# The third quarter of the output weights goes through row sums of 512 columns, and their spread follows behind it

## Chip, cores and metric

The kernel runs on one core of a Trainium2 chip. The metric is the device time of one execution in microseconds (us); less is better. Before the change the median of three runs is 381.85 us (381.62 to 381.86).

## The reference

One token `x` (1024 values) goes through two blocks, and a scalar gate mixes them:

```python
g = sigmoid((x * gate_w).sum(-1))
q = (x @ wq)                       # 32 heads of 128
scores = q @ k_cache^T * 128**-0.5 # 4 key heads, 65536 keys, 8 query heads to each
o = softmax(scores) @ v_cache      # 32 x 128 = 4096 values
a = o @ wo                         # wo: 4096 x 1024
z = gelu(x @ w_in)                 # 3584 values: z1, z2
b = (z1 * (w_sp * layernorm(z2) + b_sp)) @ w_out   # w_out: 1792 x 1024
out = g * a + (1 - g) * b          # 1024 values, bf16
```

Keys and values are 64 MB each, `wo` is 8 MB (4096 x 1024 in bf16), `wq` 8 MB, `w_in` 7 MB, `w_out` 3.5 MB. Every byte is read once.

## The kernel before

All large operands come through one ring of SBUF memory, filled by one queue of transfers that SyncE (SP) issues in the order of the list `stream`: `wq`, keys, `w_in`, keys, `w_out`, then values and keys in turn, the last values, and at the end the output weights. A load is issued as soon as the data that it overwrites has been used (`done` calls `issue`, L376 to L400). The output weights come in six loads: the first three quarters `("wo", 0..2, 0)` of 2 MB each, and the fourth quarter cut by `WO_CUT` (L357) into pieces of 5, 2 and 1 of its 8 rows per partition (1280, 512 and 256 KB).

Order on each engine is the order in which the program records its operations; a helper class counts semaphores and puts a wait ahead of an operation that needs another engine's or a transfer's result. Nothing reorders the work afterwards. What all TensorE (PE) matmuls have in common is the helper `mm` (L257): the first matmul on given weights has line L260 in the profile, and those that use the same weights again have L262.

Keys are transposed by VectorE (DVE, L502) and multiplied on PE; scores, exponentials (ScalarE, ACT) and products with values follow for pairs of pieces. Behind the last values only the tail is left (L760 to L776). It makes the product of the 4096 attention values with `wo`, on top of what the other block has left in the same sums. Four names matter in it:

- `wo_rows(i)` multiplies quarter `i` in the form of *row sums*: the attention values are the stationary operand, one column of 128 at a time, and 512 columns of `wo` move past. There are 8 columns of values in a quarter and two halves of 512, so 16 matmuls. Column group `j = c % 4` of the array writes PSUM row `32 * j`, so four matmuls on different groups can run side by side. The result is four partial rows of 1024 in the PSUM tile `scp` (first half, key `KSC(0)`); they are accumulated over the calls.
- `spread(scp, ...)` adds these four rows and lays the 1024 sums out as 8 rows of 128 in the PSUM tile `fb` (named `fbt` in the profile): one ACT copy from `scp` to SBUF (L656), and then 8 matmuls with a selecting operand in f32 (L660), each of which the profile shows as two.
- `wo_piece(i, c0, c1)` multiplies rows of quarter `i` directly into the layout of `fb`: for each of its columns of values 8 matmuls of 128 moving columns (L712), so 64 for a whole quarter.
- `spin(n)` is `n` matmuls of 128 x 512 whose result in the other half of `scp` nobody reads.

The tail in the order recorded on PE is: the last values (`pv_piece(15)`), the softmax sums `out_first(3)`, `wo_rows(0)`, the last head group's scaling `out_rest(3)`, `wo_rows(1)`, `spin(4)`, `spread`, `spin(3)`, `wo_piece(2)`, `spin(3)`, and the three pieces of `wo_piece(3)`. Then DVE casts `fb` to bf16 (L775), and SP stores 2 KB (L366).

Of the kernel before, what the change touches and what calls it, by code (L numbers as in the profile page):

```python
# [138 lines left out]
def bass_gated_mix__gqa_block_cached__mixer_gmlp__decode_kernel(  # L139
# [64 lines left out]
    def ab(name, n, o=0):  # L204
        return arena[:, OFF[name] + o:OFF[name] + o + n]
# [51 lines left out]
    def mm(e, loaded, *a, **kw):  # L257

        if not loaded:
            return e.matmul(*a, **kw)  # L260
        with nc.discard():
            one = e.matmul(*a, **kw).ins  # L262
        return e.add_instruction(dataclasses.replace(one, name=nc.get_next_instruction_name(), ldweights=False))
# [129 lines left out]
    def use(key):  # L393
        n, off, w = place[key]
        assert n < issued[0], key
        return arena[:, OFF["RING"] + off:OFF["RING"] + off + w], [("slot", x) for x in grains(off, w)]

    def done(key):
        used.add(key)
        issue()  # L400
# [253 lines left out]
    def spread(src, keys, first):  # L654
        part = ab("KT", 2048, 4096).bitcast(F32)
        P("ACT", lambda e: e.activation(part[0:97, :], src[0:97, 0:1024], ACTF.Copy), w=[("kt", 1)] + keys)  # L656

        def f(e):
            for s, b, j in SLOTS:
                ins = e.matmul(fb[32 * b:32 * (b + 1), 0:QW], e4z[0:97, 31 - j:63 - j], part[0:97, QW * s:QW * (s + 1)],  # L660
                               start=(first and s % (NW // 2) == 0), stop=False, tile_position=(0, 32 * b),
                               skip_group_check=True)
            return ins
        P("PE", f, r=["e4", ("kt", 1)], w=["fb"])
# [17 lines left out]
    def spin(n):  # L682
        def f(e):
            for k in range(n):
                ins = mm(e, k > 0, scp[:, 1024:1536], idb, ab("KT", 512), start=True, stop=True)
            return ins
        P("PE", f, r=["idb", ("kt", 0)], w=[KSC(1)])

    def wo_rows(i):
        sl, keys = use(("wo", i, 0))  # L690

        def f(e):
            for c in range(8):
                j = c % 4
                z = 31 + 32 * (8 * i + c)
                for s in range(2):
                    o = DO * c + 512 * s
                    ins = mm(e, s > 0, scp[32 * j:32 * j + 1, 512 * s:512 * (s + 1)], ovz[:, z:z + 1], sl[:, o:o + 512],
                             start=(i == 0 and c < 4), stop=(i == 1 and c >= 4), tile_position=(0, 32 * j),
                             skip_group_check=True)  # L700
            return ins
        P("PE", f, r=[("ovec", i)] + keys, w=[KSC(0)])
        done(("wo", i, 0))

    def wo_piece(i, c0=0, c1=8):
        sl, keys = use(("wo", i, c0))
        def f(e, i=i, sl=sl, c0=c0, c1=c1):
            for c in range(c0, c1):
                for s, b, j in SLOTS:
                    o = DO * (c - c0) + QW * s  # L710
                    z = 31 + 32 * (8 * i + c) - j
                    ins = e.matmul(fb[32 * b:32 * (b + 1), 0:QW], ovz[:, z:z + 32],  # L712
                                   sl[:, o:o + QW], start=False, stop=(i == 3 and c == 7),
                                   tile_position=(0, 32 * b), skip_group_check=True)
            return ins
        P("PE", f, r=[("ovec", i)] + keys, w=["fb"])
        done(("wo", i, c0))
# [48 lines left out]
    out_rest(3)  # L766
    wo_rows(1)
    spin(4)
    spread(scp, [KSC(0)], False)
    spin(3)  # L770
    wo_piece(2)
    spin(3)
    for c0, c1 in WO_CUT:
        wo_piece(3, c0, c1)
# [34 lines left out]
```

## Time and profile before

| What | Value |
|---|---|
| Runs | 381.62, 381.86, 381.85 us, median 381.85 |
| Span of the profiled execution | 380.3 us |
| Median of the runs less that span | 1.55 us |
| Busy share: PE, DVE, ACT | 62%, 54%, 6% |
| Transfer engines: mean rate, share of time with packets of the load queue | 426 GB/s, 98.9% |
| Start of the tail's cast L775 | 378.79 us |

The page does not give the whole time of the profiled execution, only its span from first to last instruction; the runs beside it lie 1.3 to 1.5 us above it. The chip's TensorE has a clock that a throttle grants, shown as a share of full speed: in this profile it is either 1.0 or 0.5, and the mean over the span is 0.838. Times below are us from the start of the span. A line of the windows view gives the stretch and its length, the busy us and instructions of each engine in it, and at the end the granted clock, the busy share of the transfer engines and their rate.

### The profile page before, as it was taken

How to read it: one execution, taken by the hardware profiler on the slowest of the kernel's cores; microseconds unless marked ns; L12 is line 12 of the kernel's file. 1: busy time of each engine (PE TensorE's matmuls, PEld its weight loads, DVE VectorE, ACT ScalarE, POOL GpSimd, SP SyncE). 2: the span in 40 equal slices, each digit the busy share in tenths (PEclk: the TensorE clock that was granted, in tenths of full speed). 3: DMA queues.
4: the chain of work that ended last, by engine and by line, in shares of the span. 5: the costliest groups of instructions: out<-in, count | busy, mean ns of one | idle time of the engine just before them, and what ended most of it. 6: DMA issues, size and time to landing. Idle time of an engine off the chain costs nothing.

```text
span 380.3 us, 2581 instructions
## 1 busy us (share of the span) xinstructions
PE 235.1 (62%) x1449; PEld 58.1 (15%) x836; DVE 204.6 (54%) x162; ACT 23.3 (6%) x24; POOL 8.4 (2%) x37
## 2 busy tenths in 40 slices
PE   0061388458558924895788138952895884739378
PEld 0010011011111200122112001220121110212015
DVE  4011496778389525965892249745774882312020
ACT  1000000010420000002200000022000000220000
POOL 5000000000000000000000000000000000000000
PEclk9998599696859985998699859995899697958689
DMA  9999999999999999999999999999999999999996
GB/s 435 427 420 400 469 388 438 441 469 431 401 414 441 441 443 427 434 410 424 477 441 434 434 434 414 415 441 441 434 407 433 445 441 441 436 403 424 419 426 262
DMA packets 4254, 162.17 MB, mean 426 GB/s; under 512 B 532, under 2 KB 532, under 8 KB 788
## 3 DMA queue, kind: packets, MB, share of 16 engines
q1 hardware_dynamic: 4208, 162.01, 98.9%
q8 instruction: 9, 0.15, 0.2%
q10 hardware_dynamic: 36, 0.00, 0.0%
q14 instruction: 1, 0.01, 0.0%
HBM read 162.01 MB, written 0.00 MB: 426 GB/s over the span
## 4 chain that ended last, share of the span: by engine, by line
DMA 56%; PE 23%; DVE 18%; ACT 1%; issue 1%; SPq 0%; ACTq 0%; DVEq 0%
DMA arena<-in_A_k_cache_dram 34%; DVE arena L502 15%; DMA arena<-in_A_wo_dram 10%; DMA arena<-in_A_v_cache_dram 8%; PE scp L260 7%; PE scp L262 6%; DMA arena<-in_B_b_sp_dram 5%; PE obt L260 4%; PE obt L262 4%; DVE arena L539 1%; PE fbt L712 1%; PE fbt L660 1%; ACT arena L534 1%; SPq L389 0%; ACTq L288 0%
## 5 line engine op out<-in xcount | busy, mean ns | idle before, releaser
L502 DVE STREAM_TRANSPOSE arena<-arena 128x2048 f32<-128x2048 f32 x64 | 143.0, 2284 | 48.2 <-DMA arena<-in_A_k_cache_dram 32.7
L260 PE MATMUL scp<-arena 128*128 128x512 bf16 (+1 forms) x275 | 112.8, 429 | 87.7 <-DVE arena L502 86.3
L262 PE MATMUL scp<-arena 128*128 128x512 bf16 (+1 forms) x279 | 113.1, 427 | 0.0
L260 PE MATMUL obt<-arena 128*64 128x512 bf16 (+2 forms) x334 | 62.9, 419 | 17.5 <-DMA arena<-in_A_v_cache_dram 17.5
L262 PE MATMUL obt<-arena 128*64 128x512 bf16 (+2 forms) x334 | 62.2, 414 | 0.0
L260 PEld LDWEIGHTS scp<-arena 128*128 128x128 bf16 (+1 forms) x275 | 27.7, 104 | 200.1 <-issue 101.3
L539 DVE STREAM_TRANSPOSE arena<-arena 128x2048 bf16<-128x2048 bf16 x7 | 16.2, 2311 | 28.5 <-PE obt L262 26.4
L534 ACT ACTIVATE arena<-arena 128x2048 bf16<-128x2048 f32 x8 | 16.0, 2002 | 218.6 <-DVE arena L531 195.6
L260 PEld LDWEIGHTS obt<-arena 128*64 128x64 bf16 (+1 forms) x334 | 18.3, 113 | 70.7 <-issue 56.1
L519 DVE TENSOR_SCALAR_CACHE_REDUCE arena<-scp 128x2048 f32<-128x2048 f32 x8 | 18.3, 2292 | 16.0 <-PE scp L262 16.0
L580 PE MATMUL mbt<-arena 128*128 128x128 bf16 x16 | 1.9, 258 | 12.6 <-DVE arena L575 12.6
L542 DVE STREAM_TRANSPOSE arena<-arena 128x1024 bf16<-128x1024 bf16 x2 | 2.5, 1246 | 12.7 <-PE obt L262 12.7
L490 POOL COPY arena<-arena 32x32 bf16<-32x32 bf16 x16 | 3.2, 203 | 234.5 <-PE scp L262 209.7
L568 DVE RECIPROCAL arena<-mbt 128x1 f32<-128x1 f32 x4 | 0.6, 139 | 14.1 <-PE mbt L563 14.1
L531 DVE TENSOR_REDUCE arena<-mbt 128x1 f32<-128x32 f32 x4 | 0.8, 192 | 13.5 <-PE mbt L528 13.5
L437 PE MATMUL mbt<-arena 1*128 1x2 bf16 x1 | 0.2, 158 | 12.3 <-DMA arena<-in_B_b_sp_dram 12.3
L439 DVE COPY arena<-mbt 128x2 f32<-128x2 f32 x1 | 0.2, 160 | 12.3 <-PE mbt L437 12.3
L775 DVE CAST arena<-fbt 36x128 bf16<-36x128 f32 x1 | 0.3, 283 | 11.0 <-PE fbt L712 11.0
L432 PE MATMUL scp<-arena 8*128 8x1 bf16 x8 | 0.7, 199 | 8.7 <-DVE arena L427 8.7
L712 PE MATMUL fbt<-arena 128*32 128x128 bf16 x128 | 4.1, 220 | 0.1
L712 PEld LDWEIGHTS fbt<-arena 128*32 128x32 bf16 x128 | 3.6, 97 | 1.6 <-DMA arena<-in_A_wo_dram 0.8
L467 DVE CAST arena<-obt 97x1024 bf16<-97x1024 f32 x1 | 1.2, 1225 | 4.9 <-PE obt L262 4.9
(91 smaller groups left out, 54.2 us busy)
## 6 DMA issues: line engine op xcount, KB each, us to landing
arena<-in_A_k_cache_dram SPq DMA_DIRECT2D x6, 4096.0 KB, 33.1
arena<-in_A_v_cache_dram SPq DMA_DIRECT2D x2, 4096.0 KB, 26.0
arena<-in_B_w_in_dram SPq DMA_DIRECT2D x1, 7168.0 KB, 30.4
arena<-in_A_wo_dram SPq DMA_DIRECT2D x3, 2048.0 KB, 33.4
arena<-in_B_w_out_dram SPq DMA_DIRECT2D x1, 3584.0 KB, 21.5
arena<-in_A_wo_dram SPq DMA_DIRECT2D x1, 1280.0 KB, 30.3
arena<-in_A_wo_dram SPq DMA_DIRECT2D x1, 512.0 KB, 31.0
arena<-in_A_wo_dram SPq DMA_DIRECT2D x1, 256.0 KB, 30.8
```

What stands on the lines that cost most here:

```text
L260: return e.matmul(*a, **kw)
L262: one = e.matmul(*a, **kw).ins
L467: P("DVE", lambda e: e.tensor_copy(psb[0:97, :], ob[0:97, :]), w=["psb", "ob"])
L490: P("POOL", lambda e, pb=pb: e.tensor_copy(vw(qpad, 24 + 32 * pb, [[QP, 4], [1, 8]], 32 * pb, 32), vw(qall, 8 * g, [[32, 4], [1, 8]], 32 * ...
L502: P("DVE", lambda e: e.transpose(ktb(i).bitcast(F32), sl[:, 4096 * p:4096 * (p + 1)].bitcast(F32)), r=keys[4 * p:4 * p + 4], w=[("kt", i % ...
L519: P("DVE", lambda e: e.tensor_scalar(scs(j), scp[:, :], 0.0, None, op0=ALU.add, op1=ALU.max, accum_out=maxc[:, j:j + 1]), w=[("sc", j % 2) ...
L534: P("ACT", lambda e: e.activation(psb2, scs(j), ACTF.Exp, bias=gcol(j // 2, K_NB), scale=SCALE, accum_out=lp[:, j:j + 1]), r=[("sc", j % 2 ...
L539: P("DVE", lambda e: e.transpose(ptsb2, psb2), r=["psb"], w=[("ptsb", 0), ("ptsb", 1)])
L542: P("DVE", lambda e: e.transpose(ptsb(n), ab("PSB", 1024, 1024 * (n % 2))), r=["psb"], w=[("ptsb", n % 2)])
L580: ins = e.matmul(mb[:, 0:128], sel[:, 128 * c:128 * (c + 1)], osc[:, 128 * c:128 * (c + 1)], start=(c == 0), stop=(c == 3))
L660: ins = e.matmul(fb[32 * b:32 * (b + 1), 0:QW], e4z[0:97, 31 - j:63 - j], part[0:97, QW * s:QW * (s + 1)], start=(first and s % (NW // 2) ...
L712: ins = e.matmul(fb[32 * b:32 * (b + 1), 0:QW], ovz[:, z:z + 32], sl[:, o:o + QW], start=False, stop=(i == 3 and c == 7), tile_position=(0 ...
```

## The change

In the tail, the third quarter goes through `wo_rows(2)` where it went through `wo_piece(2)`. `wo_rows(2)` is recorded behind `spin(4)`, and `spread` behind `wo_rows(2)`. One `spin(3)` is dropped with `wo_piece(2)`. The accumulation in `scp` is closed by the third call and not by the second (`stop`).

```diff
@@ wo_rows
-                             start=(i == 0 and c < 4), stop=(i == 1 and c >= 4), tile_position=(0, 32 * j),
+                             start=(i == 0 and c < 4), stop=(i == 2 and c >= 4), tile_position=(0, 32 * j),
@@ tail
     out_rest(3)
     wo_rows(1)
     spin(4)
+    wo_rows(2)
     spread(scp, [KSC(0)], False)
-    spin(3)
-    wo_piece(2)
     spin(3)
     for c0, c1 in WO_CUT:
         wo_piece(3, c0, c1)
```

On PE this removes 64 matmuls of 128 columns and 3 spin matmuls, adds 16 matmuls of 512 columns, and moves `spread` behind them. The instructions of DVE, ACT, POOL and SP are the same, in the same order.

## The prediction

> **What bounds the kernel now.** I read the page's rate row first (transfers busy in every slice, 426 GB/s over the span), then the chain of work that ended last, from 368 us on, then the stretches of the tail with their granted clock. The kernel is paced by its loads up to the end, so the question is what PE has left when the last load has landed. The chain's tail (start, us, what):
>
> ```profile
> 331.05 37.33 DMA arena<-in_A_wo_dram
> 368.38 0.04 issue
> 368.42 0.39 PE scp L260 x4
> ...
> 369.52 0.43 PE scp L262 x4
> 369.95 0.54 PE scp L260
> 370.49 1.28 PE scp L262 x3
> 371.77 1.24 PE fbt L660 x16
> 373.01 0.32 PE scp L260
> 373.33 0.43 PE scp L262 x2
> 373.76 1.90 PE fbt L712 x64
> ...
> 376.50 1.77 PE fbt L712 x56
> 378.27 0.01 issue
> 378.27 0.42 PE fbt L712 x8
> ...
> 378.79 0.28 DVE arena L775
> ```
>
> The reader should see that quarter 1 of wo landed at 368.38 and PE started on it 0.04 us later. From there PE is never without work: `wo_rows(1)`, `spin(4)`, spread, spin, quarter 2, spin, quarter 3. The list of transfers puts the other landings (issue plus time to landing) at 345.7 + 27.6 = 373.3 for quarter 2 and 376.4, 377.6 and 378.2 for the three pieces of quarter 3. So PE keeps pace with every landing, and only 8 matmuls and the cast follow the last.
>
> The same stretches, cut where the granted clock can change (it changes only on a grid of 3.41 us). Columns: length, PE busy, PEld, DVE, ACT, POOL, clock, transfer share, GB/s:
>
> ```profile
> 99.17:102.58 3.41, 1.79 (x22) 1.10 (x18) 1.28 (x4) 2.54 (x3) 0.00 (x0) 1.00 1.22 524
> 146.96:150.37 3.41, 2.53 (x6) 0.54 (x4) 3.01 (x2) 0.00 (x0) 0.00 (x0) 0.50 0.89 384
> 358.58:362.00 3.42, 3.27 (x16) 1.00 (x10) 0.00 (x0) 0.00 (x0) 0.00 (x0) 0.50 1.04 441
> 365.41:368.82 3.41, 0.86 (x16) 0.42 (x12) 1.78 (x4) 0.00 (x0) 0.00 (x0) 1.00 1.02 432
> 368.82:372.24 3.42, 3.42 (x22) 0.59 (x9) 0.00 (x0) 1.02 (x1) 0.00 (x0) 0.50 1.00 417
> 372.24:375.65 3.41, 3.41 (x82) 2.45 (x76) 0.00 (x0) 0.00 (x0) 0.00 (x0) 1.00 0.96 400
> ```
>
> After a stretch with PE busy 1.79 or 0.86 us of 3.41 the next stretch is at half clock. After 2.53 us at half clock it stays at half (the stretch from 150.37 has 0.50 too), after 3.27 us or more it goes to full. So a drop needs less than about half of a stretch busy, with no need for an idle one, and a rise needs somewhere between 74% and 96%. The tail before is busy throughout from 368.42, so it is at full clock from 372.24.
>
> **Part by part.** *Removed from PE:* `wo_piece(2)`, 64 x 29.6 ns = 1.90 us, and three spins, 3 x 0.215 = 0.65 us. All of it lay between the landings of quarter 2 (373.3) and quarter 3 (376.4), beside the transfers. Removing it gains nothing by itself, since the pieces of quarter 3 cannot start before they land.
>
> *Added:* `wo_rows(2)`, 16 matmuls, four side by side. At full clock four steps of 0.215 us (the four rows of `wo_rows(0)` at 364.44, 364.65, 364.87, 365.08) and 0.17 to the end of the last: 1.03 us. At half clock steps are 0.43 (369.10 to 369.52): 1.72 and about 0.2.
>
> *Moved:* spread. Before, its ACT copy (1.02 us) ran under `spin(4)`, and its 16 matmuls were done before quarter 2 landed. After, the copy waits for `wo_rows(2)`, hence for the landing at 373.3. Behind the waiting spread on PE are queued `spin(3)` and all of quarter 3; the cast and the store wait for these. On ACT nothing follows the copy. The cover is gone: `spin(4)` now stands ahead of `wo_rows(2)`. From the first spread, where nothing covered the copy: PE's last matmul ends at 99.55, the copy starts at 99.60, takes 1.02, PE starts at 100.68, so 1.13 us idle; and PE's next weight load is at 101.67, so 0.99 us for the 16 at full clock.
>
> At full clock throughout: start 373.32 (landing plus 0.04); `wo_rows(2)` 1.03 to 374.35; copy 1.13 to 375.48; spread 0.99 to 376.47; `spin(3)` 0.65 to 377.12; 40 matmuls of L712 at 29.6 ns 1.18 to 378.30; 16 more 0.47 to 378.77. There the last 8 begin; before they began at 378.27. Sum: +0.50 us, since all three pieces have landed by then.
>
> *The clock.* With spread gone from there, PE is out of work from 371.77 (end of `spin(4)` at half clock; from about 370.2 at full) to 373.32, and again for the 1.13 us of the copy. Between 371.77 and 375.48 it is busy 1.03 to 1.9 us in 3.71, so a grid stretch in there holds about 1.0 to 1.8 us: the drop's condition by the rows above. Where the clock is at half, each us does half the work. With H the us at which PE works at half clock behind 373.32, the change costs 0.50 + H/2. No row shows L712 at half clock; from both sides it is between no change (29.6 ns) and doubling (59 ns). I take doubling, because the 512-column rows double (0.215 to 0.43), and the second spread, with 0.54 us at half clock and 0.70 at full, took 1.24 against 0.99, which is doubling too.
>
> With the grid as in this profile (372.24, 375.65, 379.06): 368.82 to 372.24 is busy 2.95 us (86%, taken as enough to rise), `wo_rows(2)` runs at full clock, 372.24 to 375.65 holds 1.2 us, and 375.65 to 379.06 is at half: H = 3.41, cost 2.2 us. But the grid need not lie so in another execution. In general the clock stays at half from spread's start (375.48 to 376.40) until a stretch that lies almost wholly behind it has ended: 3.41 to 6.83 us later, or 0.5 less where 86% is enough, so 2.9 to 6.3, mean 4.6; `wo_rows(2)` at half adds up to 1.72 in some positions, about 0.4 on average. H = 5.0, cost 0.50 + 2.50 = 3.0 us. With everything at half, H = 1.72 + 1.98 + 1.29 + 64 x 0.059 = 8.8 and the cost is 4.9; with the shortest, H = 2.9, it is 1.95, and where L712 does not double 0.2 to 0.3 less.
>
> A rule of the Trainium skill speaks otherwise. "TensorE: Matmul & The Clock Gate", in the sections "Part 1: The HAM clock gate" and "Why this matters for your kernels", has the clock fall back after an idle window of about 3.4 us, and warns of gaps over about 3 us between bursts. By that rule the gaps of 1.5 and 1.1 us here would not cost the clock, and the sum would be +0.5 us. The rows disagree: the stretches with 1.79 and 0.86 us of work were not idle, and the clock dropped behind both.
>
> The profile's span is 380.3 us, with no whole time given for that execution; the median of the runs is 1.55 above it. Nothing outside the tail changes, so I add to the median: 381.85 + 3.0 = 384.85 us. A measurement here can tell about 0.2%, that is 0.76 us, from no change.
>
> **The rivals.**
>
> *The clock holds.* If the gaps are too short to drop it, or a stretch with 1.8 us counts as busy, only the serial part is left: +0.50 us, 382.35 us. For it: one stretch of the trace (133.30 to 136.72) with 1.81 us busy kept full clock. Against: the stretch in question holds 1.0 to 1.8 us, and in most grid positions under 1.3. 9%.
>
> *Faster.* PE has less to do in the tail, 0.86 instead of 2.55 us on quarter 2. If the last loads landed earlier because PE reads less beside them (385 GB/s in 374 to 375 with PE at 64 small matmuls, 459 in 367 to 368 with PE idle), up to 4.1 MB x (1/385 - 1/459) = 1.7 us would be saved on the landings from 373.3 on: at most 380.15 us. It decides only from the point where the PE chain behind quarter 2's landing, 5.9 us at full clock to the cast, gets shorter than the 4.9 us of those transfers. It is 0.5 us longer than what there was, at best. 2%.
>
> *The clock stays at half to the end.* If a rise needs a wholly busy stretch of dense work, and 128 x 32 matmuls count for less, H = 8.8: +4.9 us, 386.75 us. Against: 372.24 to 375.65, more than half of it L712, kept full clock. 9%.
>
> **How the numbers follow.** The clock drop with a rise in time has 80%: 384.85 us, its own spread from 383.5 (shortest H, L712 not doubled, and 0.3 less) to 386.1 (H = 7.5). Outside are the clock that holds, the faster case, and the half clock to the end, 20% together, so the range is 383.5 to 386.1. Slower by over 0.2%: 80 + 9 = 89%. Within 0.2%: the clock that holds, 9%. Faster: 2%.
>
> **What would show it.** Right, step by step: ACT's copy L656 starts near 374.4 to 375.3 and PE's first L660 1.1 us after `wo_rows(2)` ends; PE waits at `wo_rows(2)` for wo by 1.5 us or more; the granted clock shows 0.5 in a stretch that takes in spread and part of quarter 3; L712 starts about 59 ns apart in it; the cast L775 starts near 381.8; the last wo landing stays near 378.2. Wrong: clock 1.0 from 373 to the end with the cast near 379.3, or L712 as closely spaced at half clock, or landings that move.

## The result and the profile after

The changed kernel takes 384.87 us in the median of five runs (383.91 to 385.31) against 381.85 us (381.62 to 381.89): a ratio of 1.0078, 95% interval 1.0067 to 1.0089, so 3.0 us slower. The forecast was 384.85 us. The profiled execution took 385.31 us, with a span of 384.0.

The chain that ended last, of the changed kernel, from the landing of quarter 2 on (start, us, what):

```profile
373.42 0.04 issue
373.47 0.39 PE scp L260 x4
...
374.57 1.03 ACT arena L656
375.60 0.04 issue
375.64 1.92 PE fbt L660 x16
377.56 0.54 PE scp L260
378.11 0.85 PE scp L262 x2
378.96 3.40 PE fbt L712 x33
...
382.45 0.28 DVE arena L774
```

No transfer appears in it behind 373.42: PE and ACT alone carry the last 9 us, where before the landings set the pace. The copy now stands open in the chain. The 16 spread matmuls take 1.92 us and the 64 of quarter 3 take 3.40 (the chain counts 33 of the 64 matmuls in that piece; the timeline has all 64); at full clock, in the profile of the second kernel of the experiments, they take 1.07 and 1.91. The list of transfers gives the last landing at 347.3 + 31.1 = 378.4 against 378.2 before. Before, the weight loads of the last piece waited 0.18 us for its landing; now the last piece waits 3.5 us for PE.

The same kernel by stretches of the clock's grid (length, PE, PEld, DVE, ACT, POOL, clock, transfers, GB/s):

```profile
368.39:371.81 3.42, 3.23 (x20) 0.34 (x9) 0.00 (x0) 0.00 (x0) 0.00 (x0) 0.50 1.03 431
371.81:375.22 3.41, 1.34 (x18) 0.19 (x8) 0.00 (x0) 0.65 (x1) 0.00 (x0) 1.00 0.97 405
375.22:378.63 3.41, 2.99 (x19) 1.39 (x17) 0.00 (x0) 0.37 (x1) 0.00 (x0) 0.50 0.51 201
378.63:382.05 3.42, 3.42 (x61) 3.16 (x62) 0.00 (x0) 0.00 (x0) 0.00 (x0) 0.50 0.00 0
```

The second line is the one that matters: 1.34 us busy in 3.41, and the next stretch is at half clock. The third line is 88% busy, and the clock still did not rise behind it. It rose at 382.05, with the last of quarter 3's matmuls still to come.

The cast comes at 382.45 instead of 378.79, 3.66 us later. It adds up: 0.1 for the later landing of quarter 2 (373.42 against 373.3), 0.50 of serial work as forecast, and the half clock: spread 1.85 - 0.99 = 0.86 (to the next weight load at 377.49), spin 1.39 - 0.75 = 0.64, L712 3.40 - 1.90 = 1.50. Sum 3.6. The profiled execution is the slowest of the five.

### The profile page after: what moved, and what is told of

It reads as the page before. It is cut to its first block, busy times and chain, and to the rows that moved or that the text cites. A ratio compares the mean times of both kernels' runs of the same rounds, so it can differ in the third digit from the quotient of the medians.

```text
span 384.0 us, 2473 instructions
## 1 busy us (share of the span) xinstructions
PE 233.3 (61%) x1398; PEld 57.7 (15%) x779; DVE 204.5 (53%) x162; ACT 23.3 (6%) x24; POOL 9.4 (2%) x37
## 4 chain that ended last, share of the span: by engine, by line
DMA 62%; PE 19%; DVE 17%; issue 1%; ACTq 0%; ACT 0%; SPq 0%; DVEq 0%
DMA arena<-in_A_k_cache_dram 41%; DVE arena L502 15%; DMA arena<-in_A_v_cache_dram 9%; DMA arena<-in_A_wo_dram 7%; PE scp L260 5%; DMA arena<-in_B_b_sp_dram 5%; PE scp L262 5%; PE obt L260 3%; PE obt L262 3%; DVE arena L539 1%; PE fbt L712 1%; PE fbt L660 1%; ACTq L288 0%; ACT arena L656 0%; DVE arena L575 0%
## 5 line engine op out<-in xcount | busy, mean ns | idle before, releaser
L260 PE MATMUL obt<-arena 128*64 128x512 bf16 (+2 forms) x334 | 62.2, 414 | 18.9 <-DMA arena<-in_A_v_cache_dram 18.9
L262 PE MATMUL obt<-arena 128*64 128x512 bf16 (+2 forms) x334 | 61.6, 410 | 0.0
L660 PE MATMUL fbt<-arena 97*32 97x128 f32 x32 | 3.0, 348 | 2.3 <-ACT arena L656 2.3
## 6 DMA issues: line engine op xcount, KB each, us to landing
arena<-in_A_wo_dram SPq DMA_DIRECT2D x1, 256.0 KB, 31.1
```

## The experiments

The theory: 0.50 us is work made serial by moving spread behind quarter 2, and the rest is half clock, brought on by PE's two gaps, the wait for quarter 2 and the copy. The rivals: the serial chain costs 3 us by itself and the clock is incidental; or the last loads land later.

**Filling the gaps.** Three kernels add spin matmuls to the changed one.

```diff
     wo_rows(1)
-    spin(4)
+    spin(8)                  # e1, e2
     wo_rows(2)
+    spin(5)                  # e1, e3
     spread(scp, [KSC(0)], False)
```

> The changed tail with both gaps on PE filled by matmuls that nobody reads: spin(8) for spin(4) ahead of the wait for quarter 2, and spin(5) between wo_rows(2) and spread, under the ACT copy. Theory (0.50 us of serial work, the rest is half clock): the clock is 1.0 from about 372 us to the end, the cast starts near 379.3, time 382.3 to 382.6 us, so about 2.5 us under the changed kernel. Rival (the copy and the spread themselves cost the 3 us by standing behind the last quarters, the clock only goes along): 384.5 to 385 us, as the changed kernel. Rival (the change makes the last loads land later): 384.5 or more, with the landing of the last 256 KB near 381.

> Only the gap ahead of quarter 2 is filled (spin(8) for spin(4)); PE still idles for the ACT copy. Theory, in the form that busy time alone decides: a stretch of 3.41 us then holds at most 1.2 us of idleness, about 65% busy, the clock holds, 382.3 to 382.8 us. Rival within it (the copy's gap is enough, or the f32 matmuls of spread count for less than their time): half clock behind 375.5 in most executions, 383.5 to 385 us.

> Only the gap under the ACT copy is filled (spin(5) between wo_rows(2) and spread); PE still waits 1.5 us or more for quarter 2. Theory: the wait alone brings a stretch with under half of it busy in most positions of the grid; the clock is then at half from 373 to 375 on, but dense work resumes at 373.3 and not at 375.5, so that it can rise about 2 us sooner; the five spins at half clock take 2.15 us for the copy's 1.13. Together 383.5 to 385 us. Rival (the copy's gap is what drops the clock): as e1, 382.3 to 382.6 us.

Each had six runs, and each falls into two groups of times. Both gaps filled: 382.43, 382.51, and four from 383.87 to 384.45. Only the wait: 382.43, 382.68, and four from 384.88 to 385.23. Only the copy: 382.38, 382.52, and four from 383.92 to 384.18. (The kernel before, beside them: 381.90.) So no filling brought every run down, and the medians missed what the theory expected of the first two. But the lower groups are where the serial term alone puts them, 0.5 to 0.8 us above before. The profile of the second kernel is of its fastest run. Its chain, and the stretch that holds its copy:

```profile
373.57 0.39 PE scp L260 x4
...
374.67 1.03 ACT arena L656
375.70 0.04 issue
375.75 1.07 PE fbt L660 x16
376.81 0.32 PE scp L260
377.14 0.43 PE scp L262 x2
377.57 1.91 PE fbt L712 x64
...
379.57 0.28 DVE arena L774
```

```profile
372.70:376.12 3.42, 1.91 (x26) 0.57 (x18) 0.00 (x0) 1.02 (x1) 0.00 (x0) 1.00 0.96 397
```

From quarter 2's landing on, this is the changed kernel's program, instruction for instruction. Only the clock differs: the stretch with the copy held 1.91 us of work, not 1.34, and full clock stayed. From the first weight load at 373.57 to the cast it takes 6.00 us; in the changed kernel's profile the same steps take 8.98. Hence 3.0 us of the 9 are clock. That refutes the rival of the serial chain, and since quarter 2 landed later here than there (373.53 against 373.42), also that of later loads.

Why eight spins do not always fill the wait is seen in the third kernel, whose profile is of its slower group (four spins, as in the changed kernel):

```profile
367.21:370.62 3.41, 2.06 (x23) 0.52 (x13) 1.08 (x3) 0.00 (x0) 0.00 (x0) 1.00 1.02 432
370.62:374.04 3.42, 0.53 (x9) 0.19 (x8) 0.00 (x0) 0.00 (x0) 0.00 (x0) 1.00 0.96 400
374.04:377.45 3.41, 3.41 (x21) 0.10 (x1) 0.00 (x0) 1.02 (x1) 0.00 (x0) 0.50 0.81 327
```

The grid lay so that full clock lasted through `wo_rows(1)`. The spins then took 0.2 us each, PE was done at 370.8, and it idled 2.9 us. A filler of a fixed number of matmuls is half as long when the clock is high. That this is also what splits the runs of the first two kernels was not seen, since no profile shows their slower groups.

**The move alone and the form alone.** The first takes the kernel before and puts spread behind `wo_piece(2)`, with one `spin(3)` dropped. The second keeps spread and spin where they were before, lets `wo_rows(2)` start fresh sums, and spreads these a second time.

```diff
     spin(4)                  # e4: the move alone, from the kernel before
-    spread(scp, [KSC(0)], False)
-    spin(3)
     wo_piece(2)
+    spread(scp, [KSC(0)], False)
     spin(3)
```

> The kernel before with spread moved behind wo_piece(2) and one spin(3) dropped, so the move without the new form. The ACT copy stays covered. Theory: at full clock 373.32 + 1.90 + 0.99 + 0.65 and 56 x 0.0296 put the last 8 matmuls at 378.52, 0.25 us later than before; but the wait for quarter 2 is there as in the changed kernel, so the clock drops in most positions and H of 3 to 5 us adds 1.5 to 2.5: 382.5 to 384.5 us. Rival (the new form or its serial copy is what costs): 381.9 to 382.2 us.

Twelve runs, again two groups: six from 381.74 to 381.98, six from 383.32 to 383.78; ratio 1.0020 (1.0008 to 1.0032). The lower group equals before, so there the move costs 0.1 us or less, even under the 0.25 expected; that these runs had full clock is not shown, since none of them has a profile. The upper group pays 1.4 to 1.9 us, and its profile shows the clock:

```profile
370.81:374.22 3.41, 0.85 (x30) 0.85 (x32) 0.00 (x0) 0.00 (x0) 0.00 (x0) 1.00 0.95 395
374.22:377.63 3.41, 3.41 (x57) 3.10 (x50) 0.00 (x0) 0.00 (x0) 0.00 (x0) 0.50 0.77 310
```

So without any of the new form the move brings the idle wait and with it half clock; but with dense work from 373.4 on, the clock rises after one stretch.

```diff
     spin(4)                  # e12: the form alone, from the changed kernel
+    spread(scp, [KSC(0)], False)
+    spin(3)
     wo_rows(2)               # starts fresh sums
     spread(scp, [KSC(0)], False)
     spin(3)
```

> The new form for quarter 2 without the move: spread and spin(3) stay behind spin(4) as in the kernel before, wo_rows(2) starts fresh sums behind them, and a second spread of its own follows. The work ahead of quarter 2's landing is then that of the kernel before, so PE does not idle there for more than 0.5 us at half clock and 1.7 us at full; the serial copy, spread and spin behind the landing are those of the changed kernel. Theory (0.50 us serial, the rest from PE idling ahead of quarter 2): 382.3 to 382.6 us in most executions, a few near 384 where the copy's 1.1 us in a stretch with spread drops the clock. Rival (the serial chain behind the landing costs 3 us by itself, or its own gap drops the clock as a rule): 384 to 385 us in most.

Eleven runs, 382.17 to 382.96, median 382.42 against 381.82: 0.60 us, ratio 1.0016 (1.0007 to 1.0025), one group. The copy's gap is open here, 1.1 us of it, and the serial chain behind quarter 2 is that of the changed kernel. With the earlier work back ahead of the landing, that chain costs its 0.5 us and little more. In its profile the stretch with the open copy (the second line) holds 2.27 us of work, and full clock stays behind it to the end:

```profile
369.35:372.76 3.41, 3.08 (x23) 1.40 (x17) 0.00 (x0) 1.02 (x1) 0.00 (x0) 0.50 0.96 399
372.76:376.17 3.41, 2.27 (x29) 0.57 (x17) 0.00 (x0) 1.02 (x1) 0.00 (x0) 1.00 0.96 394
```

With the copy filled and the wait open (the third kernel), four of six runs fell into the upper group; with the wait filled by earlier work and the copy open, there was no upper group in eleven. This answers which gap does the damage: the wait for quarter 2.

**Without the last spin.** The changed kernel without the `spin(3)` behind spread:

> The changed kernel without the spin(3) between spread and quarter 3. Theory: where the clock is at full, spread ends at 376.5, quarter 3's first piece has just landed, and the 0.50 us of serial work are gone: 381.9 us; where it is at half (most executions, both gaps are as in the changed kernel) 1.3 us are saved at most: 383 to 384 us. Rival (the spin keeps the clock from staying at half, and its loss costs more than its time): 385 us or more.

383.81 to 384.10 in five runs, median 383.96 (before 381.84). About 0.9 us of the 3.0 are saved, in the range expected at half clock. No run reached the 381.9 of full clock. In its profile the stretch from 370.36 to 373.77 has PE busy 0.53 us, and both behind it are at half clock.

**Taking the wait away.** Quarter 2 is loaded in four pieces of 512 KB, and `wo_rows(2)` is cut to match, so that PE has real work during the wait at either clock.

```diff
-    for i in range(3):
+    for i in range(2):
         load([("wo", i, 0)], rows(A_wo, i, 8), WO_AT[i])
+    for c0 in range(0, 8, 2):
+        load([("wo", 2, c0)], rows(A_wo, 2, 8)[:, DO * c0:DO * (c0 + 2)], WO_AT[2] + DO * c0)
...
     wo_rows(1)
-    spin(4)
-    wo_rows(2)
+    spin(4)                  # e9: spin(1)
+    for c0 in range(0, 8, 2):
+        wo_rows(2, c0, c0 + 2)
+        if c0 < 6:
+            spin(3)          # e9: spin(1)
+    spin(5)
     spread(scp, [KSC(0)], False)
     spin(3)                  # e9: dropped
```

> The changed kernel with quarter 2 of wo loaded in four pieces of 512 KB, wo_rows(2) split to match, spin(3) behind each of the first three, and spin(5) under the ACT copy. PE then has work at every landing, at either clock, and does not run out of it for more than about half of any 3.41 us. Theory (0.50 us of serial work, the rest half clock from the wait for quarter 2): the clock is 1.0 through the end in nearly all executions; behind the last landing of quarter 2 only four of the 16 matmuls are left, so the last 8 matmuls start within 0.1 us of the last landing: 381.8 to 382.2 us, no two groups of times. Rival (the order itself costs, whatever the clock): 383 us or more. Rival (smaller loads are slower): the last 256 KB land later than 378.6.

384.15 to 384.48, median 384.35: one group, but 2.5 us above before. Its clock was full from 371.89 to the end. What failed was the amount of filling. Quarter 2's last piece had landed at 373.6, and PE reached it at 375.99, behind its own spins:

```profile
373.95 0.32 PE scp L260
374.28 0.43 PE scp L262 x2
374.71 0.31 PE scp L260 x2
...
375.99 0.31 PE scp L260 x2
```

Every piece costs 1.28 us this way, as long as the piece takes to land, so a late start is never made up. The last 256 KB landed at 378.6, 0.4 us later than before, but PE reached quarter 3 only at 379.46, so that later landing is not what costs here. The kernel is no test of the order; it shows that spins in front of a chain without slack cost their full time.

> The cut quarter with less filling, since the 12 matmuls of the first four spins and three per piece kept PE 2.3 us behind the landings at full clock: spin(1) behind wo_rows(1), spin(1) behind each of the first three pieces, spin(5) under the ACT copy, and no spin(3) behind spread. Theory: PE takes each piece as it lands (last start 373.6 to 374.0), spread ends near 376.4, no serial cost is left and the clock holds: 381.8 to 382.2 us, in one group. Rival (a stretch half busy with one-column weights is not enough to hold the clock): some executions at 383 to 384 us. Rival (the order itself costs): 383 us or more in all.

Eleven runs, 381.87 to 382.16, median 382.00 against 381.90: ratio 1.0003 (0.9994 to 1.0012), no difference that can be told. Its chain is paced by landings again (L714 is the line of `wo_piece` in this kernel):

```profile
376.74 0.14 issue
376.87 1.76 PE fbt L714 x56
378.64 0.01 issue
378.65 0.42 PE fbt L714 x8
```

The stretch in which the last pieces of quarter 2 land holds 2.58 us of work at full clock:

```profile
371.02:374.43 3.41, 2.58 (x15) 0.54 (x9) 0.00 (x0) 0.10 (x1) 0.00 (x0) 1.00 1.04 423
```

So the new order with the new form costs nothing that can be told where quarter 2 comes in pieces and no spin stands behind spread: PE works while the quarter lands, and only the last fourth of `wo_rows(2)` is left behind it.

**The old order without spins.** The kernel before without its ten spin matmuls:

> The kernel before without any of its ten spin matmuls in the tail: the old form and the old order, but the same wait for quarter 2 with PE idle. Theory (half clock is most of the cost, whatever the form): at full clock no change, 381.8 us; where the wait drops the clock, wo_piece(2) and part of wo_piece(3) run at 53 ns a matmul and the cast comes 1 to 2 us later, 383 to 384 us; so two groups of times, or all in the upper one. Rival (the form and the order cost, not the clock): 381.7 to 382.0 us in all executions.

Eleven runs, 381.68 to 382.18, median 381.86, ratio 1.0000 (0.9991 to 1.0009). The two groups that I expected are not there. The profile has full clock from 364.40 to the end, with stretches no busier than these:

```profile
367.81:371.22 3.41, 1.97 (x30) 0.95 (x24) 0.69 (x2) 1.02 (x1) 0.00 (x0) 1.00 1.00 425
371.22:374.64 3.42, 1.77 (x54) 1.51 (x52) 0.00 (x0) 0.00 (x0) 0.00 (x0) 1.00 0.99 411
```

Spread, in its old place, shortens the wait to 1.65 us, and the second stretch held with 52%. My expectation also left out that `wo_piece(2)` has 3.1 us between the landings of quarter 2 and quarter 3 and needs 1.9 us, or 3.4 at half clock (what the 64 matmuls of quarter 3 took in the changed kernel). By these numbers half clock there would be nearly free in the old order. The runs do not tell how many of these executions had it.

**What lifts and holds the clock.** To see whether spread's f32 matmuls count less than their time, two kernels add a long run of one kind behind the last matmul of the kernel before.

> The kernel before with 120 matmuls of spread's kind (f32, 97 rows, 32 x 128 columns, two column groups in turn) added behind the last matmul; they add zeros or leftovers to columns of fb that nobody reads. The question is whether such work holds the clock: the stretch with spread in the changed kernel was busy 88% at half clock and the clock did not rise, where other stretches with 79% did. If busy time alone counts: full clock throughout, 240 x 62 ns, 396.5 to 397.5 us. If this kind counts for less: the clock falls to 0.5 within 7 us and stays there, 402 to 409 us.

> The control to the f32 run: 480 bf16 matmuls of quarter 3's shape (128 rows, 32 x 128 columns, two column groups in turn) added behind the last matmul of the kernel before, into columns of fb that nobody reads. If busy time alone counts, or the f32 kind alone counts for less: full clock throughout, 480 x 29.6 ns, 395.5 to 397 us. If all matmuls that use a quarter of the array count for less: half clock after some us, 401 to 408 us.

394.93 and 395.35 us: both kinds held 1.0 in every stretch to the end, at 54 ns (f32; 62 had been expected) and 28 ns (bf16) from one to the next. A third kernel runs both from half clock, with PE idle ahead of each:

> The kernel before with work behind its end that nobody uses: PE idles while DVE makes five copies of 128 x 2048, then 150 f32 matmuls of spread's kind (300 in the profile), then five copies again, then 480 bf16 matmuls of quarter 3's shape; the time is of no interest, the clock in the two runs is. If busy time alone lifts the clock: both runs start at 0.5 and are at 1.0 after 3.4 to 6.8 us. If the f32 kind counts for less: the first run stays at 0.5 to its end (about 33 us), the second rises. If all 32-column matmuls count for less: neither rises.

```profile
385.38:388.79 3.41, 3.25 (x32) 2.81 (x34) 0.11 (x1) 0.00 (x0) 0.00 (x0) 0.50 0.00 0
388.79:392.20 3.41, 3.41 (x36) 2.95 (x34) 0.00 (x0) 0.00 (x0) 0.00 (x0) 0.50 0.00 0
392.20:395.62 3.42, 3.42 (x66) 3.42 (x64) 0.00 (x0) 0.00 (x0) 0.00 (x0) 1.00 0.02 5
```

The f32 run does lift the clock, but not in a stretch that it fills to 95%; it took a full one. The bf16 run rose behind its first full stretch as well; the one ahead of that held only 0.96 us of it, so this kernel does not set the two kinds apart.

## Why the prediction was right, and where it was off

- *Direction and size.* Both held: 3.0 us forecast, 3.0 measured. The mechanism is shown by runs: the same instructions behind quarter 2 take 6.0 us at full clock and 9.0 in the changed kernel's profile.
- *The serial term, 0.50 us.* Confirmed by the form alone (0.60) and by the lower groups of the three filled kernels (0.5 to 0.8).
- *Gaps drop the clock.* Confirmed, with the wait ahead of quarter 2 as the main one. The rule that the prediction set against the rows, that an idle window of about 3.4 us is needed (the Trainium skill, "TensorE: Matmul & The Clock Gate", "Part 1: The HAM clock gate"), would have given +0.5 us; the stretches with 0.53, 0.85 and 1.34 us of work, none of them idle, all lost the clock.
- *H = 5.0 us at half clock.* In the profile it was 6.4, from 375.64 to 382.05, and 0.50 + 6.4 / 2 = 3.7 us is close to what the cast lost there (3.66). The step that failed is "86%, taken as enough to rise": by it half clock would have ended at 378.63, with H = 3.0, but the 88% of that stretch, 1.92 of its 2.99 us spread, were not enough. Only the other value, up to 6.83 us from spread's start, holds the 6.4.
- *L712 doubles to 59 ns.* From one start to the next it takes 53 ns at half clock and 28 at full (the changed kernel and the second filled one), 1.9 times, so nearly that. The 59 was too high because the 29.6 had the end of the last matmul in it.
- That the median came out so close is partly luck: 5.0 is a mean over positions of the grid, only one of the five executions shows its own, and that one lost 3.5 us (385.31 against 381.85).
- *The rival "the clock holds", 382.35 us.* None of the five runs of the changed kernel came near it; two of six did in each filled kernel, at 382.4 to 382.7.
- *The rival "half clock to the end", 386.75 us.* In the profile half clock lasted nearly as long as it says, until 0.3 us ahead of the end of quarter 3. But `wo_rows(2)` ran at full clock, so H was 6.4 and not 8.8, and the slowest run took 385.31.
- *The rival "faster".* The landings did not move forward (last wo at 378.4 against 378.2), and fewer matmuls beside them brought nothing.

Not settled: what besides busy time decides a drop or a rise, and how the times of the changed kernel spread over the grid's position, since only one of its executions has a trace of its clock.

## What to carry to other kernels

Ahead of a removal, ask what the removed or moved work covered: here a spread and its spin that ran while a load was under way kept PE's clock up, and moving them behind the load both opened a gap and put the whole chain where nothing hides it. Between a late landing and the end, count serial steps and not instructions: 51 fewer matmuls, and 3 us more. Filling a wait with a fixed count of dummy matmuls fits one clock only; cut the load and let real work arrive in pieces.

## What the hardware showed that was not expected

- Busy time, as the profile shows it, does not alone decide the rise. At half clock, a stretch 79% busy (the value products of the last pieces, changed kernel) and one 88% busy (row sums and spins, the kernel with the two cold runs) lifted the clock:

```profile
358.15:361.57 3.42, 2.70 (x14) 0.79 (x8) 0.00 (x0) 0.00 (x0) 0.00 (x0) 0.50 1.00 426
368.31:371.72 3.41, 3.00 (x19) 0.34 (x9) 0.00 (x0) 1.02 (x1) 0.00 (x0) 0.50 1.01 423
```

- One 88% busy of which 1.92 us were spread, and one of f32 matmuls alone 95% busy, did not lift it; one 90% busy with 1.5 us of spread in it (the form alone) did. A stretch of 1.77 us with spread in it held full clock in one kernel (the old order without spins), and one of 1.79 us lost it in another (the kernel before). What is counted besides the time is not shown.
- The small matmuls gain a little less than twofold from the full clock: 53 ns to 28 ns from one to the next in quarter 3.
- A high clock can undo itself: at full clock PE finished the four spins in half the time and then idled 2.9 us ahead of quarter 2 (the third filled kernel), where with half clock it idled 1.4 us (the changed kernel).
